# Batch 0's softmax and norm reworked at the head of a fused attention and feed-forward kernel: squares from products of the states, transposes by TensorE, a new first order

## The chip, the cores and the metric

The kernel runs on one core of one Trainium2 chip. A core has TensorE (PE, matmuls[...]), VectorE (DVE), ScalarE (ACT), GpSimd (POOL) and SyncE (SP), each with its own instruction queue that is worked off in order, and 16 DMA engines that all queues share. The metric is the device time of one launch in microseconds (us), as the median of several runs. The profiled execution has a span, from the first to the last instruction of the core, and a time that is a little longer.

## What is computed

The reference, cut to what matters (all in float32; eight batches, eight heads of 64, 512 tokens and 32 states per batch):

```python
def _attn_ref(x, state):                     # x (8, 8, 512, 64), state (8, 8, 32, 64)
    scale = 1.0 / np.sqrt(D)
    a = softmax(scale * x @ state.T)         # with max, and sum + 1e-09
    xread = a @ state
    a2 = softmax(scale * state @ x.T)
    sread = a2 @ x
    return np.concatenate([xread, sread], axis=2)

def _moe_ref(x, w_gate, w_val, w_out, rms_g):   # x (4352, 512), widths 512 -> 1536 -> 512
    rms = np.sqrt(np.mean(x * x, axis=-1, keepdims=True) + 1e-06)
    xn = x / rms * rms_g
    g = xn @ w_gate
    return (g / (1.0 + np.exp(-g)) * (xn @ w_val)) @ w_out
```

The norm needs, for each token, the mean square of `xread` over all heads. The weights arrive as 64-bit floats.

## The kernel before

The attention output of the tokens is never formed. A token's row of `xread` is `a` (32 values per head) times the states, so the kernel multiplies the states into the weights (`own_weights`) and applies the softmax values `a` to the result. What it needs of `xread` itself is its length, for the norm.

Of the eight batches, batch 0 is done in a first stretch of its own, together with the conversion of the weights from 64 bit and with the attention of batch 1. From batch 1 on each batch is one period, and the states are last. What stands on PE, DVE, ACT, POOL and SP, and in which order, is written out by hand: strings of letters (`ORDER` for the first stretch, then `FIRST`, `PERIOD`, `LAST`, `STATES`), where each letter takes one step of one generator. In `ORDER`, `a` and `s` are the reads of batch 0 (`tokens_read`, `states_read`), `A` and `S` those of batch 1, `e` and `d` the two halves of the weight conversion (`exponents` on ACT, `values` on DVE), `v` is `own_weights`, `h`, `t` and `u` are the hidden layer of batch 0 (matmuls on PE, silu on ACT, gating on DVE), `p` is its projection, `c`, `k` and `w` prepare batch 1, and `z` is `keep_awake`, one 128x256 matmul that computes nothing (L1149).

The weights come in 18 pieces: for each of six pairs of hidden blocks one of `w_gate`, one of `w_val` and one of `w_out`. A piece is loaded as raw 64-bit data (`load_piece`, four pieces ahead), takes three ACT steps (L234, L236, L239) and four DVE steps (L260, L263, L267, L272), each over 128x1024 elements; piece 0 is cut in two halves. `own_weights` (L567) needs the converted `w_gate` and `w_val` of its pair, `project_as_ready` (L817) the converted `w_out`.

Batch 0's path runs so. Scores: the states are transposed (L307, copied by DVE at L310), x is transposed in four chunks (L318, copied by ACT at L320), and the scores (L345) come out with the 32 states of four heads on the partitions, in two PSUM banks, `e` = 0 and 1. DVE transposes them in 32x32 blocks (L354) so that the states lie along the free dimension, takes the maximum (L414) and subtracts it (L416); ACT takes the exponential (L418); DVE sums (L426), inverts (L428, L429), scales (L431) and transposes back (L433) into `aT_s`. ACT keeps a copy of the scores for the states' own read (L358).

Norm: PE forms the token reads (L440, `aT_s` times the states) in four banks, ACT squares them (L447), DVE adds the four (L450), PE sums over the partitions (L367), DVE adds the small constant (L371), POOL takes the power -1/2 (L289), PE spreads the result over the rows (L296), and DVE scales `aT_s` by it (L453). Only then can the first matmul of the hidden layer (L610) start. The matmuls of L610, L817 and L567 then fill PE up to the first product of batch 1 (L714).

The start of the loads: SP issues the states of batch 0, chunks 1 and 3 of x, `rms_g` and then the weight pieces; ACT issues chunks 0 and 2 of x:

```python
    load_state(0)
    load_x(0, nc.scalar, nc.sync)
    nc.sync.dma_start(out=rms_g, in_=moe_rms_g.rearrange("(i p) -> p i", p=P))
    load_piece(0)
```

PSUM has eight banks; the pools are `aps` and `vps` (two each, tiles `at` and `pv`), `fx` (two), `fy` and `fz` (tiles `f`).

Of the kernel before, what the change touches and what calls it, by code (L numbers as in the profile page):

```python
# [22 lines left out]
    "zzzzzzzzzzazadaaaaaaaaazzzdzzzzzzeaeeaaaaadaadeeaaaaeeezdeazdzzzzzzadeeeaadaadzz"  # L23
    "zzzzzzzaaaaaddadzzzzvvvaaedzaAAdaaassdAAAAaAAeeAaAhtddddehehhuppedddddvtduppeeee"
    "ddvvdddeeeedAAddhhtuhhpeAddeApAtddeesvuvddveApdddhheedtupddeeehtAAAddhueeeddsApA"
    "AAdpepvvevAsddddedddphtsssseeehuhAdtssddpdshuedeedpvvvAeApdeAehtdhhAueddppAdddtA"
    "eeddpAheuSSAAAeAAvAvvpehhtSSddhdAAASSpAtuSShSSSdkAuwwsSSSpcpcskpwckkkkkkkkpwkkwc"
    "wwww"
# [29 lines left out]
def kernel(  # L58
# [137 lines left out]
    def load_piece(k):  # L196
        if k >= len(pieces):
            return
        src = pieces[k]
        if src.dtype == F32:  # L200
            return
        raw[k] = raws.tile([P, 8 * P, 2], I32, name="raw")
        out_ = raw[k].rearrange("p (a f) two -> p a (f two)", a=src.shape[1])
        for a in parts(k):
            nc.sync.dma_start(out=out_[:, a], in_=src[:, a].bitcast(I32))

# [85 lines left out]
    def along_rows(ri, n):  # L292

        rp = aps.tile([P, NC, P], F32, name="at")
# [7 lines left out]
    def scores(b, packed, soft):  # L302
# [8 lines left out]
        yield "step"  # L311

# [40 lines left out]
        for e in range(2):  # L353
# [7 lines left out]
        soft.update(st=stT, e=eS)  # L361

    def rms_on_array(b, sq):

        sp = aps.tile([P, NC], F32, name="at")
        for c in range(NC):
            TE.matmul(out=sp[:, c:c + 1], lhsT=sq[:, 0, P * c:P * c + P], rhs=ones,  # L367
                      start=True, stop=True)
# [6 lines left out]
        rp = along_rows(ri, NC)  # L375
# [27 lines left out]
    def tokens_read(b):  # L403
# [6 lines left out]
        def along(t, e):  # L410
            return t[:, e].unsqueeze(2).to_broadcast([P, S // Ns, Ns])

        for e in range(2):
            VE.reduce_max(out=m1[:, e], in_=eS[:, e], axis=AXX)  # L414
            yield
            VE.tensor_tensor(out=eS[:, e], in0=eS[:, e], in1=along(m1, e), op=ALU.subtract)  # L416
# [8 lines left out]
        for e in range(2):  # L425
# [7 lines left out]
            VE.transpose(out=aT_s[b][:, e], in_=eS[:, e].rearrange("p k n -> p (k n)"))  # L433
# [3 lines left out]
        reads = [(aps, vps)[j // 2].tile([P, S], F32, name=("at", "pv")[j // 2]) for j in range(4)]  # L437
        for j in range(4):
            for e in range(2):
                TE.matmul(out=reads[j][D * e:D * e + D, :],  # L440
                          lhsT=packed[Ns * j:Ns * j + Ns, e, :],
                          rhs=aT_s[b][Ns * j:Ns * j + Ns, e],
                          start=True, stop=True)
        yield
        sq = one.tile([P, 4, S], F32, name="sq", tag="xT")
        for i, j in enumerate((2, 3, 0, 1)):
            SE.activation(out=sq[:, i, :], in_=reads[j], func=ACTF.Square, scale=DM ** -0.5)  # L447
            yield "step" if i == 3 else None
        for i, j in ((0, 1), (2, 3), (0, 2)):
            VE.tensor_tensor(out=sq[:, i, :], in0=sq[:, i, :], in1=sq[:, j, :], op=ALU.add)  # L450
            yield
        rp = yield from (rms_on_array if b < 2 else rms_on_blocks)(b, sq)
        VE.tensor_tensor(out=aT_s[b], in0=aT_s[b],  # L453
                         in1=rp.unsqueeze(1).to_broadcast([P, 2, S]), op=ALU.mult)
# [100 lines left out]
    def own_weights(b, mp):  # L555
# [4 lines left out]
        def products():  # L560
            w = w_sb.pop(b * (NM // 2) + mp)
            for e in range(2):
                pv.append(vps.tile([P, 4 * P], F32, name="pv") if b and mp % 2 == 0 else
                          aps.tile([P, 4 * P], F32, name="at"))
# [601 lines left out]
    parts_0, banks_0 = {}, []  # L1166
    load_state(0)
    load_x(0, nc.scalar, nc.sync)
    nc.sync.dma_start(out=rms_g, in_=moe_rms_g.rearrange("(i p) -> p i", p=P))
    load_piece(0)  # L1170
    for k in range(1, RAW_AHEAD):
        load_piece(k)
# [76 lines left out]
```

## Time and profile before

| | us |
|---|---|
| median of three runs | 762.73 |
| lowest, highest | 762.08, 765.21 |
| the profiled execution | 762.78 |
| its span | 760.5 |
| PE busy | 747.2 (98%) |
| DVE busy | 600.3 (79%) |
| ACT busy | 351.1 (46%) |
| POOL busy | 294.0 (39%) |
| first hidden product of batch 0 (L610) starts | 36.27 |
| first product of batch 1 (L714) starts | 136.78 |

The times of engines are from the page of the profile, the two starts from the timeline of PE. A float32 matmul appears as two records, so "x8" in a row stands for four matmuls. In the timeline a row gives the start, the length, the engine, the line, the tiles and in brackets how long the engine had been idle and what released it. The busy share of PE contains the matmuls of `keep_awake`, which are work for the profile but not for the result.

### The profile page before, as it was taken

To read this page: it belongs to the slowest core of one execution; us is meant where nothing else is said; L and a number is where in the kernel's file an instruction comes from. 1 tells how busy PE (TensorE), PEld (TensorE's weight loads), DVE (VectorE), ACT (ScalarE), POOL (GpSimd) and SP (SyncE) were. 2 spreads that over 40 slices of the span, in tenths; PEclk is the share of its full clock that TensorE was granted. 3 is DMA by queue.
4 is the path that set the end of the run, shared out by engine and by line. 5 is a ranking of instruction groups with operands and counts; after the bars stand their busy time and mean duration, and the time that the engine had idled before them with its cause. 6 is when DMAs were issued, how large, how long until landed. Compare 5 with 4: busy or idle time off the path is not lost.

```text
span 760.5 us, 14354 instructions
## 1 busy us (share of the span) xinstructions
PE 747.2 (98%) x5608; PEld 595.3 (78%) x5608; DVE 600.3 (79%) x1000; ACT 351.1 (46%) x548; POOL 294.0 (39%) x379
## 2 busy tenths in 40 slices
PE   8899999999899999999999999999999999999998
PEld 6534435678778798879877997889788987899997
DVE  3999997679956898589947994799579975787961
ACT  4898974553225532654155424553355236411220
POOL 2000002893675325542374038312843266323700
PEclk9999999999999999999999999999999999999999
DMA  9787754695576266834774376617662756133411
GB/s 291 214 277 264 289 214 162 231 305 178 195 234 242 56 244 214 297 78 181 256 245 151 125 267 219 222 40 306 217 228 39 293 184 241 56 90 119 140 56 28
DMA packets 61890, 146.15 MB, mean 192 GB/s; under 512 B 15744, under 2 KB 32640, under 8 KB 54912
## 3 DMA queue, kind: packets, MB, share of 16 engines
q1 hardware_dynamic: 48704, 125.78, 47.3%
q10 hardware_dynamic: 13120, 19.47, 9.0%
q8 instruction: 44, 0.72, 0.4%
q14 instruction: 22, 0.18, 0.1%
HBM read 116.46 MB, written 28.77 MB: 191 GB/s over the span
## 4 chain that ended last, share of the span: by engine, by line
PE 88%; DVE 8%; POOL 1%; ACT 1%; issue 1%; DMA 0%; SPq 0%; ACTq 0%; POOLq 0%; DVEq 0%
PE f L714 36%; PE f L1017 27%; PE f L817 6%; PE pv L610 5%; PE at L567 3%; PE pv L567 2%; PE f L880 2%; PE at L345 1%; PE f L1149 1%; PE at L509 1%; PE at L440 1%; DVE hb L1076 1%; DMA out_dram<-kept 0%; PE at L296 0%; DVE hb L790 0%
## 5 line engine op out<-in xcount | busy, mean ns | idle before, releaser
L714 PE MATMUL f<-aT_s,v 128*128 128x256 f32 x504 | 119.6, 382 | 0.0
L714 PEld LDWEIGHTS f<-aT_s,v 128*128 128x128 f32 x504 | 94.5, 190 | 24.8 <-issue 9.2
L777 DVE TENSOR_TENSOR g<-g,f 128x512 f32<-128x512 f32 x84 | 57.3, 685 | 42.6 <-PE f L714 38.6
L1043 POOL TENSOR_TENSOR kept<-kept 128x256 f32<-128x256 f32 x28 | 23.1, 826 | 175.0 <-DVE kept L1057 173.6
L714 PE MATMUL f<-aT_t,vs 128*128 128x256 f32 x336 | 87.2, 383 | 0.3 <-ACT g L761 0.3
L1027 ACT COPY kept<-f 128x512 f32<-128x512 f32 (+1 forms) x56 | 29.7, 532 | 124.8 <-PE f L1017 83.0
L1017 PE MATMUL f<-w,h 128*128 128x128 f32 x588 | 74.6, 276 | 1.0 <-DVE h L1067 1.0
L714 PEld LDWEIGHTS f<-aT_t,vs 128*128 128x128 f32 x336 | 62.4, 190 | 16.0 <-POOL vs L594 4.2
L1017 PEld LDWEIGHTS f<-w,h 128*128 128x128 f32 x588 | 69.6, 192 | 5.4 <-issue 4.1
L768 ACT ACTIVATE hb<-g 128x1024 f32<-128x1024 f32 x42 | 44.5, 1058 | 56.7 <-DVE g L777 56.6
L594 POOL TENSOR_TENSOR vs<-v 128x256 f32<-128x256 f32 x42 | 31.7, 755 | 80.4 <-ACT v L579 80.4
L289 POOL TENSOR_TENSOR ri<-ss,mhalf 128x4 f32<-128x4 f32 x8 | 10.4, 1295 | 124.5 <-DVE ss L371 114.6
L766 ACT COPY g<-f 128x512 f32<-128x512 f32 x42 | 24.6, 586 | 44.5 <-PE f L714 44.5
L714 PE MATMUL f<-aT_t,v 128*128 128x256 f32 x168 | 43.5, 381 | 1.6 <-DVE c L777 1.6
L817 PE MATMUL f<-wo,hb 128*128 128x512 f32 x96 | 44.4, 600 | 0.0
L610 PE MATMUL pv<-aT_s,v 128*128 128x512 f32 x96 | 43.7, 597 | 0.3 <-ACT t L616 0.3
L714 PE MATMUL f<-aT_s,vs 128*128 128x256 f32 x168 | 43.6, 382 | 0.0
L790 DVE TENSOR_TENSOR hb<-hb,c 128x512 f32<-128x512 f32 (+1 forms) x48 | 36.9, 768 | 8.0 <-ACT hb L768 7.3
L790 DVE TENSOR_TENSOR hb<-hb,f 128x512 f32<-128x512 f32 (+1 forms) x48 | 31.0, 646 | 15.0 <-PE f L714 15.0
L1017 PE MATMUL f<-wo,h 128*128 128x128 f32 x336 | 42.2, 275 | 0.0
L1017 PE MATMUL f<-wo,hb 128*128 128x128 f32 x336 | 42.1, 275 | 0.0
L777 DVE TENSOR_TENSOR c<-c,f 128x512 f32<-128x512 f32 (+1 forms) x48 | 31.2, 650 | 12.6 <-PE f L714 12.5
(183 smaller groups left out, 1689.1 us busy)
## 6 DMA issues: line engine op xcount, KB each, us to landing
w_m<-w_d SPq DMA_DIRECT2D x48, 1024.0 KB, 5.9
w<-t_d SPq DMA_DIRECT2D x49, 576.0 KB, 5.4
out_dram<-kept SPq DMA_DIRECT2D x56, 128.0 KB, 2.1
raw<-in_moe_w_val_dram SPq DMA_DIRECT2D x6, 1024.0 KB, 5.5
raw<-in_moe_w_out_dram SPq DMA_DIRECT2D x6, 1024.0 KB, 7.1
w_d<-w_m SPq DMA_DIRECT2D x6, 1024.0 KB, 4.9
x_b<-in_x_dram SPq DMA_DIRECT2D x6, 1024.0 KB, 7.5
x_d<-xB ACTq DMA_DIRECT2D x6, 1024.0 KB, 4.2
```

The source lines that it names most:

```text
L567: TE.matmul(out=pv[e][Ns * j:Ns * j + Ns, :], lhsT=stT_g[b][D * e:D * e + D, j, :], rhs=w[D * e:D * e + D, j].rearrange("p m k f -> p (m k ...
L594: GE.tensor_tensor(out=vs[:, 0], in0=a21, in1=a22, op=ALU.add)
L610: TE.matmul(out=to[0], lhsT=lhs(i, k), rhs=r, start=(i == 0), stop=(i == len(rhs) - 1))
L714: TE.matmul(out=ps[:, i, 0:half], lhsT=l[:, i, :], rhs=r, start=(start and i == 0 and k == 0), stop=(k == len(lhs) - 1), skip_group_check= ...
L766: SE.copy(gates(q)[1], q["x"][:, :, 0:half])
L768: SE.activation(out=hb[:, 2 * mp:2 * mp + 2, 0:n].rearrange("p m (c t) -> p m c t", c=2), in_=q["g"][:, :, :, 0:half], func=ACTF.Silu if s ...
L777: VE.tensor_tensor(out=to, in0=to, in1=q[ps][:, :, 0:half], op=ALU.add)
L790: VE.tensor_tensor(out=part, in0=part, in1=val, op=ALU.mult)
L817: TE.matmul(out=banks[r], lhsT=hb[:, m, P * r:P * r + P], rhs=wo[:, m, :], start=(m == 0), stop=(m == NM - 1))
L1017: TE.matmul(out=to[half][:, slot, :], lhsT=lhs[:, k, :], rhs=rhs[:, k, :], start=(fresh and n in (0, 4) and k == 0), stop=(k == QM - 1), s ...
L1027: SE.copy(k[:, 4 * i:4 * i + 4 - i], banks[name][i])
L1043: GE.tensor_tensor(out=k[:, 1:3], in0=k[:, 0:1].to_broadcast([P, 2, QD]), in1=k[:, 1:3], op=ALU.add)
```

## The change

Five things are changed, all for batch 0 and in the first stretch.

1. The mean square of a token's read is taken without forming the read. With G = states times states, transposed (32x32 per head, divided by 512, the `gram` tile), the sum of squares of a head is the sum over its states of a * (G a). PE forms G once (8 small matmuls) and then G a (`ga`), DVE multiplies by `aT_s`, and the sum over the partitions takes both halves (8 matmuls of one column). The four squares on ACT and the three additions on DVE are gone for batch 0.
2. The four transposes in 32x32 blocks on DVE are replaced for batch 0 by 128x128 transposes on PE. The first ones read the copy that ACT makes of the scores; maximum and subtraction then read PSUM. The second ones are copied to `aT_s` by ACT.
3. The last scaling of `aT_s` is done in two halves.
4. The first half of weight piece 0 is issued on SP ahead of all else; ACT issues chunks 0 and 1 of x, SP chunks 2 and 3; `rms_g` comes after piece 1.
5. `ORDER` is dealt anew, and some PSUM tiles of batch 0 come from other pools. 13 `z` instead of 10 stand ahead of the first transpose, 14 instead of 31 after the scores; four transposes of x of batch 1 stand after the first hidden products instead of before them.

The other order strings are as before. The core of the diff:

```diff
@@ scores
+        if b == 0:
+            gp = [vps.tile([P, Ns], F32, name="pv") for e in range(2)]
+            for j in range(4):
+                for e in range(2):
+                    st = stT[D * e:D * e + D, j, :]
+                    TE.matmul(out=gp[e][Ns * j:Ns * j + Ns, :], lhsT=st, rhs=st, start=True, stop=True)
+            yield
+            gram = soft["gram"] = x_0.tile([P, 2, Ns], F32, name="gram")
+            for e in range(2):
+                VE.tensor_scalar(gram[:, e], gp[e], 1.0 / DM, None, op0=ALU.mult)
+            yield "step"
...
-        for e in range(2):
+        soft.update(st=stT, e=eS, raw=[eS[:, e] for e in range(2)])
+        for e in range(2) if b == 0 else ():
+            SE.copy(sS[:, e].rearrange("p c t -> p (c t)"), sp[e])
+            yield
+            tp = vps.tile([P, NC, P], F32, name="pv")
+            for c in range(NC):
+                TE.transpose(out=tp[:, c, :], in_=sS[:, e, c, :], identity=ident)
+            soft["raw"][e] = tp.rearrange("p c (j n) -> p (c j) n", n=Ns)
+            yield "step" if e else None
+        for e in range(2) if b else ():
             VE.transpose(out=eS[:, e].rearrange("p k n -> p (k n)"),
@@ tokens_read
-            VE.reduce_max(out=m1[:, e], in_=eS[:, e], axis=AXX)
+            VE.reduce_max(out=m1[:, e], in_=soft["raw"][e], axis=AXX)
             yield
-            VE.tensor_tensor(out=eS[:, e], in0=eS[:, e], in1=along(m1, e), op=ALU.subtract)
+            VE.tensor_tensor(out=eS[:, e], in0=soft["raw"][e], in1=along(m1, e), op=ALU.subtract)
...
+            tp = aps.tile([P, NC, P], F32, name="at")
+            for c in range(NC):
+                TE.transpose(out=tp[:, c, :], identity=ident,
+                             in_=eS[:, e, 4 * c:4 * c + 4].rearrange("p j n -> p (j n)"))
+            yield
+            SE.copy(aT_s[b][:, e], tp.rearrange("p c t -> p (c t)"))
             yield "step"
...
+        if b == 0:
+            sq = one.tile([P, 2, S], F32, name="sq", tag="xT")
             for e in range(2):
+                ga = vps.tile([P, S], F32, name="pv")
+                for j in range(4):
+                    here = slice(Ns * j, Ns * j + Ns)
+                    TE.matmul(out=ga[here, :], lhsT=soft["gram"][here, e, :], rhs=aT_s[b][here, e],
+                              start=True, stop=True)
+                yield
+                VE.tensor_tensor(out=sq[:, e, :], in0=aT_s[b][:, e], in1=ga, op=ALU.mult)
+                yield "step" if e else None
...
-        VE.tensor_tensor(out=aT_s[b], in0=aT_s[b],
-                         in1=rp.unsqueeze(1).to_broadcast([P, 2, S]), op=ALU.mult)
+        for e in (slice(0, 2),) if b else (slice(0, 1), slice(1, 2)):
+            VE.tensor_tensor(out=aT_s[b][:, e], in0=aT_s[b][:, e],
+                             in1=rp.unsqueeze(1).to_broadcast([P, e.stop - e.start, S]), op=ALU.mult)
@@ loads
+    halves = load_parts(0)
+    next(halves, None)
     load_state(0)
-    load_x(0, nc.scalar, nc.sync)
+    load_x(0, nc.scalar, nc.scalar, nc.sync, nc.sync)
+    for _ in halves:
+        pass
+    load_piece(1)
     nc.sync.dma_start(out=rms_g, in_=moe_rms_g.rearrange("(i p) -> p i", p=P))
-    load_piece(0)
-    for k in range(1, RAW_AHEAD):
+    for k in range(2, RAW_AHEAD):
         load_piece(k)
```

`load_parts(k)` is `load_piece(k)` as a generator that issues one part of the piece at each step.

## Prediction

> **What bounds the kernel now.** I read the page first: TensorE (PE) is busy 98% of the span and has 88% of the chain that ended last. Such a share leaves almost nothing to win except where PE is kept busy with work that nobody needs, so I then asked for the busy time by stage. The order of instructions per engine, compared between the two kernels, is the same from the first product of batch 1 on (the group `f<-aT_s,v` of L714); all that changes lies before it. In the trace that first product starts at 136.78 us.
>
> ```profile
> core 0: us, PE busy (x) PEld busy (x) DVE busy (x) ACT busy (x) POOL busy (x), PEclk, DMA share, GB/s
> 0.00:36.30 36.30, 31.93 (x179) 23.20 (x179) 24.54 (x42) 22.95 (x32) 6.00 (x28) 1.00 0.92 264
> 36.30:136.80 100.50, 100.17 (x512) 42.35 (x511) 92.42 (x121) 79.67 (x100) 6.18 (x8) 1.00 0.68 240
> ```
>
> From 36.30 to 136.80 us PE works 100.17 of 100.50 us: that stage cannot shrink unless matmuls go. Before 36.30 PE is busy too, but with what? The timeline of PE tells:
>
> ```profile
> 8.15 0.27 PE L307 MATMUL at<-ident,rows 128*128 128x128 f32 x1
> ...
> 11.79 1.09 PE L345 MATMUL at<-xT,stT 64*32 64x512 f32 x16 [0.68 <-ACT xT L320]
> 12.81 11.49 PE L1149 MATMUL f<-ident 128*128 128x256 f32 x52
> ...
> 33.93 0.65 PE L296 MATMUL at<-ident,ri 128*128 128x128 f32 x4 [0.45 <-POOL ri L289]
> 34.41 0.60 PE L318 MATMUL at<-ident,x_b 128*128 128x128 f32 x4
> 35.69 0.66 PE L318 MATMUL at<-ident,x_b 128*128 128x128 f32 x4 [0.68 <-ACT xT L320]
> 36.27 3.70 PE L610 MATMUL pv<-aT_s,v 128*128 128x512 f32 x8
> ```
>
> The L1149 matmuls (52 records, 26 matmuls, 0.442 us each) are the idle-time filler. So the first 36 us are the latency of batch 0's softmax and norm, and VectorE (DVE) sets it. Its timeline, from scores to the scaled softmax that L610 waits for:
>
> ```profile
> 12.97 1.31 DVE L354 STREAM_TRANSPOSE eS<-at 128x512 f32<-128x512 f32 x2 [1.84 <-PE at L345]
> ...
> 24.62 0.70 DVE L433 STREAM_TRANSPOSE aT_s<-eS 128x512 f32<-128x512 f32 x1
> ...
> 28.75 1.29 DVE L450 TENSOR_TENSOR sq<-sq 128x512 f32<-128x512 f32 x2
> ...
> 35.01 1.21 DVE L453 TENSOR_TENSOR aT_s<-aT_s,at 128x1024 f32<-128x1024 f32 x1
> ```
>
> DVE has no idle note between those lines: 22 us of back-to-back work, a good part of it the conversion of weight pieces (L260 to L272). Last the waits of PE inside the dense stage, and SP's queue at the start:
>
> ```profile
> PE pv L610 <- ACT t L616: 0.3, 1, 0.3
> ```
>
> ```profile
> 2.57 1.06 SPq L137 DMA_DIRECT2D x_b<-in_x_dram  x2
> 4.17 1.07 SPq L1169 DMA_DIRECT2D rms_g<-in_moe_rms_g_dram  x1
> 5.29 1.20 SPq L205 DMA_DIRECT2D raw<-in_moe_w_gate_dram  x2
> ```
>
> The norm weights' DMA takes 1.07 us to issue where its neighbours take about 0.5; the wait of SP there is 0.5 us, for the first chunk of x, so that chunk landed at about 4.7 us.
>
> **What the skill says.** "TensorE: Matmul & The Clock Gate", Part 1, has PE at half clock until about 3.4 us of sustained work and again after an idle window of about 3.4 us. The trace agrees for the start: the filler runs at about 0.8 us a matmul until some 5 us and at 0.44 later; no hole before L610 is over 1 us, so no return to the slow clock is seen. "DMA: Bandwidth & Descriptors", section on queues and rings, says that each DMA engine takes turns between the rings packet by packet; a large load on SP therefore delays one that ScalarE (ACT) issues at the same moment. No run here shows that case yet. DVE reads of PSUM (g<-g,f, 685 ns) and of SBUF (0.69 us) cost the same in this trace, so moving a source to PSUM is put at nothing.
>
> **The change, part by part.** Instructions on DVE follow each other at less than their duration; from the timeline I take 0.61 us for a 128x512 op (0.68 if it needs the one before), 1.14 for 128x1024, 0.34 to 0.7 for `top`, 0.45 for the z pair with its reciprocal.
>
> *Start.* 13 filler matmuls stand ahead of the first transpose instead of 10, at 0.442: stT's copy moves from 8.46 to 9.79 us and ends at 10.08. The Gram matmuls are new: 8 of 32x32. The trace has no such shape; L509's small tiles bound it below (64 records in 1.10 us, so 0.3 for 16), L345's tiles of the same position with 16 times the columns above (1.09 us for 16 records). I take 0.5 to 0.9 (the latency of the last one and of its semaphore included), so x's transposes begin at 10.55 to 10.95 instead of 8.85. From there to L345 was 2.94 us, to the scores in PSUM 1.18 more: 14.7 to 15.1, against 12.97. Loss so far 1.7 to 2.1 us. The first half weight piece is what this buys: it has landed by about 6 us (4.7 us after issue, as before), so its three ACT and first two DVE steps are done before x; before, DVE waited for it to 9.97 and ACT's share stood at 11.63 to 13.9.
>
> *Scores to softmax.* Gone from DVE: four 512-wide transposes (2 x 0.65 of scores, 2 x 0.62 of aT) and three additions (1.9), 4.5 us. Added: two products with the Gram result (1.2), one maximum moved ahead (0.6), two tiny evictions off the path. The transposes now run PE -> ACT or ACT -> PE: sS copy 0.57, four transposes 0.45, and eS is read from PSUM. DVE then goes without a hole: sS max 15.35 to 15.75, max e0 15.95, subtract 16.6, max e1 17.2, ex 17.85, subtract 18.45, stT_g 19.05, sum 19.25, weight 19.85, z 20.45, scale e0 20.9, sum 21.5, z 22.1, scale e1 22.6, `top` 23.2, man 23.9, sq e0 25.05, ex 25.65, sq e1 26.8, weight 27.4, ss 28.55 (low ends; high ends are 0.4 later). The aT copy of e1 is queued on ACT behind two weight steps (1.15 each) and comes at 24.8, its product at 26.4, ahead of sq e1: covered by 0.4 us. Without that cover each late us of ACT is a us of the path.
>
> *Norm to L610.* POOL's power 1.0 us, four transposes 0.6: ready at 30.3. But DVE has `top`, sS max, man, stT of batch 1 and ex of piece 2 queued ahead (3.8 us from 28.55): the scaling starts at 32.35, its first half (now split) ends at 33.0, and the first hidden product starts at 33.05 to 33.45, mean 33.25, against 36.27. That is 3.0 us earlier. Four transposes of x of batch 1 (0.53) now come after it instead of before, which gives 0.5 back; the 0.34 us wait for `t` goes, since ACT's table load and first silu (36.0 to 36.6) end before the second pair needs the bank (37.6).
>
> *Dense stage.* The same matmuls as before otherwise: 100.17 + 0.53 = 100.7 from 33.25 gives 133.95 for the first batch-1 product, against 136.78: 2.8 us. This needs DVE and ACT to stay ahead. DVE starts its conversions 2.7 us earlier with the same list after it, so the last w_m of the sixth pair, which before ended at 111.2 for a matmul at 111.94, ends near 108.3 for one at 109.1. ACT has two places where DVE waits for it (0.6 us each, at the seventh silu and at the 14th piece): inside the 0.8 us of slack.
>
> *Loads.* SP puts half a piece (about 0.55 us of issue) ahead of the state and two chunks of x; ACT now issues chunks 0 and 1. The rotation of eight DMA semaphores makes chunk 3 wait for chunk 0's landing, 4.7 us before and up to 1.3 later now (512 KB at the 400 GB/s the timeline shows once large rows flow): issue at about 6, landing (3.4 to 5.2 after issue) at 9.5 to 11.5. Its transposes are due at 12.5. So it is hidden by 1 us or more. All later loads shift by under 1 us and have over 3.
>
> *Later batches.* Same order; their waits are relative to PE, so the 2.8 us stays. 762.78 less 2.8 is 760.0 for the profiled execution; the median shown is 0.05 lower: 759.9. The span would be 757.7.
>
> **Rivals.**
> (1) More than that: every unknown at its low end (Gram matmuls 0.3, ops at 0.6 throughout, scaling at 31.5 to 31.9) and the c3 transposes falling into waits of PE. The first product at 32.2, gain 4.1: 758.6. For it: the DVE sums made with single durations came out about 1.5% above the stretch from 35 to 110 us. Against: the path has few places with play.
> (2) The start eats it: chunk 3 lands at about 14.5 instead of 11, because big packets stand between the small ones of x. Then L610 moves 2 us and some 0.8 us are left: 761.9. Against: the margin above.
> (3) Slower: PE's clock. Between the transposes of e1 and the first hidden product PE has holes (about 1.7 us before the second Gram product, shorter ones after), with little filler between. If PE drops to half clock there, it enters the dense stage slow; each window of 3.4 us costs 1.7 us of matmuls. Two windows cost 3.4, a third of a us more for the transposes on the path: 759.9 + 3.8 = 763.7. It decides from the second window; over 0.5% slower needs four. Against: the longest hole is half a window.
> (4) The dense stage starves: a pair of w_m late by more than 0.8 us. Each us is one us; 1.5 late gives 761.4.
>
> **How the numbers follow.** 0.5% (3.8 us) is about what a measurement of this kernel can tell from no change. Chances: forecast 0.53, (1) 0.24, (2) and (4) 0.14, (3) 0.09, of which 0.05 beyond 0.5%, to which (4) adds 0.01. The forecast's own range is 759.2 to 760.8; with (1), (2) and most of (4) it reaches from 757.8 to 762.3. Faster by over 0.5% is (1) and the edge of the forecast: 0.28. Slower 0.06, within 0.5% 0.66.
>
> **What would show it.** The first transpose of the states at 9.5, the scores' matmuls at 13.7, the first scaled aT at 33, the first hidden product at 33.3, no wait of PE over 0.5 us up to the first product of batch 1, and that at 134. A wait of PE for x at 11 to 14 us shows (2); a low granted clock or 0.8 us fillers after 20 us shows (3); PE waiting for w_m shows (4). If the first product comes at 134 and the span shrinks by something else, the later batches are not as independent as I took them to be.

## The result, and the profile after

| | before | after |
|---|---|---|
| median of six runs each on one chip | 763.65 | 759.85 |
| lowest, highest | 762.08, 765.21 | 759.33, 760.79 |
| the profiled execution | 762.78 | 759.33 |
| its span | 760.5 | 757.5 |
| first hidden product of batch 0 (L610, now L658) | 36.27 | 33.82 |
| first product of batch 1 (L714, now L762) | 136.78 | 134.30 |
| from the first of these to the second | 100.51 | 100.48 |

The ratio of after to before is 0.9953, with a 95% interval from 0.9934 to 0.9972. The forecast was 759.9. The two medians lie 3.8 us apart, the two profiled spans 3.0 and the first hidden products 2.45: which of these is the gain is taken up in the part on the prediction.

The busy time by stage of the changed kernel shows at once where the gain lies. The columns are the window, its length, then busy time and number of instructions of PE, of the weight loads (PEld), of DVE, ACT and POOL, then the granted clock of PE, the DMA share and GB/s.

```profile
0.00:33.60 33.60, 28.25 (x184) 19.64 (x184) 21.77 (x38) 21.26 (x29) 7.15 (x28) 1.00 0.96 256
33.60:134.20 100.60, 100.49 (x516) 42.90 (x514) 92.24 (x121) 80.26 (x101) 7.50 (x9) 1.00 0.70 249
```

The second stretch is as full as before and as long as before; the first is shorter. So the question is the first 34 us only. The timeline of PE in the changed kernel:

```profile
9.80 0.27 PE L310 MATMUL at<-ident,rows 128*128 128x128 f32 x1
10.45 0.29 PE L321 MATMUL pv<-stT 64*32 64x32 f32 x16 [0.39 <-DVE stT L313]
10.68 1.09 PE L333 MATMUL at<-ident,x_b 128*128 128x128 f32 x8
...
13.83 1.09 PE L360 MATMUL at<-xT,stT 64*32 64x512 f32 x16 [0.67 <-ACT xT L335]
...
26.08 1.06 PE L477 MATMUL pv<-aT_s,gram 32*32 32x512 f32 x8 [0.45 <-ACT aT_s L467]
27.07 2.24 PE L391 MATMUL f<-ones,sq 128*128 128x1 f32 x16
...
31.29 0.65 PE L299 MATMUL pv<-ident,ri 128*128 128x128 f32 x4
...
33.82 3.70 PE L658 MATMUL pv<-aT_s,v 128*128 128x512 f32 x8
```

The Gram matmuls (L321) take 0.29 us, and from the states' transpose to the scores 4.0 us pass, against 3.6 before (8.15 to 11.79). The scores are therefore 2.0 us later than before, and the first hidden product is nevertheless 2.45 us earlier: between the two, 4.5 us were saved. DVE, whose list of work stands between the two:

```profile
4.96 0.53 DVE L263 TENSOR_SCALAR top<-raw 128x512 int32<-128x512 int32 x1 [4.96 <-DMA raw<-in_moe_w_gate_dram]
...
15.63 0.69 DVE L513 TENSOR_REDUCE m<-sS 128x1 f32<-128x512 f32 x1 [2.11 <-ACT sS L370]
...
29.34 0.16 DVE L396 TENSOR_SCALAR ss<-f 128x4 f32<-128x4 f32 x1
...
31.95 1.21 DVE L270 SCALAR_TENSOR_TENSOR ex<-raw,ex 128x1024 int32<-128x1024 int32 x1
33.08 1.28 DVE L500 TENSOR_TENSOR aT_s<-aT_s,pv 128x512 f32<-128x512 f32 x2
```

The first half of weight piece 0 is there at 4.96 us. From 15.63 to the scaling DVE has no idle note in its timeline. The sum of squares (`ss`) comes at 29.34 against 32.62 before; the norm is then ready on PE at about 32, but the scaling (L500) stands behind five steps of other work and starts at 33.08.

Some 2.4 of the 4.5 us were not saved but moved. Four conversion steps of piece 0 that stood behind the scores in the kernel before (L267, L272, L260 and L263, at 15.49, 16.69, 18.69 and 19.39, 2.42 us in sum) now stand ahead of them (at 11.04, 11.76, 12.37 and 12.82), in time that DVE spends waiting anyway. The rest is what fell away on DVE, transposes and additions, less what came in.

Of the waits of PE from 33 to 136 us one line is left, and the wait for `t` that the kernel before had is gone:

```profile
PE at L333 <- ACT xT L335: 0.2, 1, 0.2
```

### The profile page after: what moved, and what is told of

It is laid out like the page before. It is cut to its first block, busy times and chain, and to the rows that moved or that the text cites. A ratio compares the mean times of both kernels' runs of the same rounds, so it can differ in the third digit from the quotient of the medians.

```text
span 757.5 us, 14370 instructions
## 1 busy us (share of the span) xinstructions
PE 743.8 (98%) x5618; PEld 592.5 (78%) x5618; DVE 599.3 (79%) x998; ACT 350.1 (46%) x546; POOL 295.2 (39%) x379
## 4 chain that ended last, share of the span: by engine, by line
PE 91%; DVE 7%; issue 1%; ACT 1%; POOL 0%; DVEq 0%; POOLq 0%
PE f L762 37%; PE f L1065 28%; PE f L865 6%; PE pv L658 6%; PE at L615 3%; PE pv L615 3%; PE f L928 2%; PE f L1197 1%; PE at L556 1%; PE at L360 1%; PE at L486 1%; DVE hb L1124 1%; PE at L299 0%; DVE hb L838 0%; DVE eS L456 0%
## 5 line engine op out<-in xcount | busy, mean ns | idle before, releaser
L762 PE MATMUL f<-aT_s,v 128*128 128x256 f32 x504 | 119.6, 382 | 0.0
L762 PEld LDWEIGHTS f<-aT_s,v 128*128 128x128 f32 x504 | 94.5, 190 | 24.8 <-issue 8.4
L1091 POOL TENSOR_TENSOR kept<-kept 128x256 f32<-128x256 f32 x28 | 23.1, 824 | 174.9 <-DVE kept L1105 173.8
L762 PE MATMUL f<-aT_t,vs 128*128 128x256 f32 x336 | 87.1, 383 | 0.0
L762 PEld LDWEIGHTS f<-aT_t,vs 128*128 128x128 f32 x336 | 62.5, 190 | 15.3 <-POOL vs L642 4.2
L762 PE MATMUL f<-aT_t,v 128*128 128x256 f32 x168 | 43.5, 381 | 1.6 <-DVE c L825 1.6
L658 PE MATMUL pv<-aT_s,v 128*128 128x512 f32 x96 | 43.9, 595 | 0.1
L762 PE MATMUL f<-aT_s,vs 128*128 128x256 f32 x168 | 43.6, 382 | 0.0
L838 DVE TENSOR_TENSOR hb<-hb,c 128x512 f32<-128x512 f32 (+1 forms) x48 | 36.7, 764 | 8.0 <-ACT hb L816 7.2
```

Source lines behind the costliest of these rows:

```text
L658: TE.matmul(out=to[0], lhsT=lhs(i, k), rhs=r, start=(i == 0), stop=(i == len(rhs) - 1))
L762: TE.matmul(out=ps[:, i, 0:half], lhsT=l[:, i, :], rhs=r, start=(start and i == 0 and k == 0), stop=(k == len(lhs) - 1), skip_group_check= ...
L838: VE.tensor_tensor(out=part, in0=part, in1=val, op=ALU.mult)
L1091: GE.tensor_tensor(out=k[:, 1:3], in0=k[:, 0:1].to_broadcast([P, 2, QD]), in1=k[:, 1:3], op=ALU.add)
```

## The experiments

The theory to be tested has two parts. *The head alone sets the time*: everything after the first hidden product runs as before, so a change of its start passes one to one into the time. *DVE's queue sets the head*, with what it waits for. The rival is the third one of the prediction: PE's clock. In all kernels the same function is computed, and none leaves work out. HP is the start of the first hidden product and FB that of the first product of batch 1, both from the timeline of PE in the profiled execution. The mean granted clock (by the record of cores) belongs to that execution; median and ratio to before, with its interval, are over all timed runs (their number in brackets). The ratio is the one on record and is not the quotient of the two medians: for e12 that would be 760.54 to 762.17, or 0.998.

| kernel | HP | FB | FB−HP | clock | median | ratio to before |
|---|---|---|---|---|---|---|
| e1 squares as before | 39.61 | 139.96 | 100.35 | 0.993 | 765.33 (20) | 1.0029 [1.0017, 1.0042] |
| e2 transposes as before | 38.63 | 139.01 | 100.38 | 0.991 | 763.90 (12) | 1.0007 [0.9994, 1.0021] |
| e3 loads as before | 36.89 | 137.30 | 100.41 | 0.996 | 761.86 (20) | 0.9989 [0.9977, 1.0001] |
| e4 10 fillers at the start | 33.61 | 133.98 | 100.37 | 0.998 | 760.00 (7) | 0.9953 [0.9934, 0.9973] |
| e5 4 fillers more in the holes | 34.94 | 135.43 | 100.49 | 1.0 | 760.91 (21) | 0.9976 [0.9966, 0.9987] |
| e6 e4 and e5 together | 33.74 | 134.23 | 100.49 | 0.999 | 760.55 (11) | 0.9980 [0.9967, 0.9992] |
| e7 e1 with 8 fillers | 35.64 | 136.05 | 100.41 | 0.998 | 761.39 (20) | 0.9990 [0.9983, 0.9997] |
| e8 e2 with 16 fillers | 35.97 | 136.47 | 100.50 | 1.0 | 762.21 (12) | 0.9995 [0.9983, 1.0008] |
| e9 scaling one step ahead | 33.55 | 134.37 | 100.82 | 1.0 | 760.57 (21) | 0.9975 [0.9965, 0.9985] |
| e10 e4 with one filler | 32.51 | 133.00 | 100.49 | 0.998 | 758.06 (6) | 0.9933 [0.9911, 0.9956] |
| e11 before, new loads | 36.47 | 136.96 | 100.49 | 0.999 | 762.37 (20) | 1.0003 [0.9991, 1.0015] |
| e12 changed, again | 34.73 | 135.09 | 100.36 | 0.998 | 760.54 (15) | 0.9962 [0.9948, 0.9975] |

e1 to e4, e5 to e8 and e9 to e12 ran on one chip each, with medians of before of 762.43, 761.96 and 762.17. In thirteen of the fourteen traces FB−HP lies between 100.35 and 100.51 (e9 is treated below), while HP goes from 32.5 to 39.6. Up to FB the first part of the theory is shown: a change of HP passes on unchanged. From FB to the end of the span it holds less well. There the fourteen traces take 623.0 to 625.3 us, a spread nearly as large as the gain. In e5 and e7 some 1.5 us of it lie behind the last matmul, in the issue of the last output transfers (first line the changed kernel, second e5); in e10 a stretch of slow clock lies in a later batch, as is shown below.

```profile
754.52 0.85 ACTq L1180 DMA_DIRECT2D out_dram<-h  x2
756.26 2.40 ACTq L1180 DMA_DIRECT2D out_dram<-h  x2
```

One thing more moves HP by some tenths. The same 13 fillers at the start take 8.50 us in the first trace of the changed kernel and 8.09 in e12, which has the same program, so that the states' transpose starts at 9.80 in the one and at 9.39 in the other. Where two traces are compared below, this start is given if it differs.

### Parts of the change taken out: e1, e2, e3

e1 forms the token reads again, squares them on ACT and adds on DVE; the order string was adapted.

```diff
-        if b == 0:
-            gp = [vps.tile([P, Ns], F32, name="pv") for e in range(2)]
...
-                VE.tensor_tensor(out=sq[:, e, :], in0=aT_s[b][:, e], in1=ga, op=ALU.mult)
+        for i, j in enumerate((2, 3, 0, 1)):
+            SE.activation(out=sq[:, i, :], in_=reads[j], func=ACTF.Square, scale=DM ** -0.5)
+            yield "step" if i == 3 else None
+        for i, j in ((0, 1), (2, 3), (0, 2)):
+            VE.tensor_tensor(out=sq[:, i, :], in0=sq[:, i, :], in1=sq[:, j, :], op=ALU.add)
```

> The changed kernel with the squares of before: eight matmuls form batch 0's reads, ACT squares four banks, DVE adds three times; the Gram products are gone, all else is as changed. Main theory (the moment at which the first hidden product can start sets the whole time, and DVE and ACT queues set that moment): four squares on ACT (2.1 us) and three additions (1.9) stand in for two products (1.2), and the additions wait for the squares. First hidden product 1.0 to 2.0 us later than the changed kernel's 33.82 us, first product of batch 1 and the span later by the same, so about 761 us. Rival (the gain is from the new order and the early load, the arithmetic being covered by other work): within 0.3 us of the changed kernel.

e2 puts the four transposes back on DVE and keeps the rest; here too the order string was adapted. Of the code, the part on the second two:

```diff
-            tp = aps.tile([P, NC, P], F32, name="at")
-            for c in range(NC):
-                TE.transpose(out=tp[:, c, :], identity=ident,
-                             in_=eS[:, e, 4 * c:4 * c + 4].rearrange("p j n -> p (j n)"))
-            yield
-            SE.copy(aT_s[b][:, e], tp.rearrange("p c t -> p (c t)"))
+            VE.transpose(out=aT_s[b][:, e], in_=eS[:, e].rearrange("p k n -> p (k n)"))
```

> The changed kernel with the block transposes of DVE for batch 0 in place of those of TensorE; the Gram products and the loads stay. Main theory: the first two fall into a hole of DVE at 13.5 to 15.6 us but push the first maximum of sS behind them (0.6), the last two (1.25) are added to DVE's closed queue, while the ACT copies and their latency go: first hidden product 1.2 to 2.0 us later than 33.82, the span by the same. Rival (DVE is not what sets that moment): no later, or earlier by up to 0.5 us, since a copy of ACT and the waits of TensorE for it are gone.

e3 has the old order of loads under the new order of everything else.

```diff
-    halves = load_parts(0)
-    next(halves, None)
     load_state(0)
-    load_x(0, nc.scalar, nc.scalar, nc.sync, nc.sync)
-    for _ in halves:
-        pass
-    load_piece(1)
+    load_x(0, nc.scalar, nc.sync)
     nc.sync.dma_start(out=rms_g, in_=moe_rms_g.rearrange("(i p) -> p i", p=P))
+    load_piece(0)
+    load_piece(1)
```

> The changed kernel with the loads issued as before (states, x, rms_g, then the weights; x dealt in turn to ACT and SP). Main theory: the first half piece lands at about 10 us, and the copy of the transposed states is queued on DVE behind its first two steps (1.1 us), so it comes at 11.1 instead of 10.11; ACT's three steps end at 12.1 in front of the first copy of x. First hidden product 0.8 to 1.2 us later, the span by the same. Rival (the early load itself buys nothing, the order does): within 0.3 us.

All three moved HP further than had been expected from DVE's durations: 5.8, 4.8 and 3.1 us. The timeline of PE of e1 shows why (in the changed kernel the 16 records of the own-weights product, L591 here, take 1.09 us and four filler records 1.03):

```profile
30.77 1.87 PE L379 MATMUL f<-ones,sq 128*128 128x1 f32 x8 [3.88 <-DVE sq L472]
...
32.74 1.91 PE L1173 MATMUL f<-ident 128*128 128x256 f32 x4
34.59 1.96 PE L591 MATMUL f<-w_m,stT_g 64*32 64x512 f32 x16
```

After a hole of 3.88 us the four filler records take 1.91 us instead of 1.03, and L591 1.96 instead of 1.09. The busy time by windows of e1 gives the clock:

```profile
28.10:31.50 3.40, 0.73 (x4) 0.73 (x4) 2.58 (x4) 3.37 (x5) 0.00 (x0) 0.50 0.90 297
31.50:34.90 3.40, 3.40 (x19) 2.48 (x26) 2.23 (x5) 0.77 (x1) 1.02 (x1) 0.50 0.90 330
34.90:38.30 3.40, 3.40 (x25) 1.82 (x10) 1.66 (x3) 0.59 (x1) 0.00 (x0) 0.50 0.00 0
38.30:41.70 3.40, 3.18 (x14) 1.81 (x13) 3.37 (x5) 3.20 (x5) 0.00 (x0) 0.99 0.16 18
```

The clock is 0.50 for three whole windows, then full. e2 has it too, for four windows, from 23.1 to 36.7 us, after a hole of 3.77 us:

```profile
23.67 1.93 PE L460 MATMUL pv<-aT_s,gram 32*32 32x512 f32 x8 [3.77 <-DVE aT_s L450]
```

e3 has two separate stretches, from 11.3 to 14.7 and from 31.7 to 35.2. So rival 3 is no mere possibility, and e1 to e3 measure two things at once: the part of the change, and the clock that the removed part had kept up. They don't tell the worth of a part at full clock.

### The same parts with the clock kept up: e5, e7, e8

Fillers were put into the holes: in e5 two ahead of the second Gram product and two ahead of the sum over the partitions, in e7 eight after the token reads, in e8 sixteen at three places. The code of e7 and e8 is that of e1 and e2; only letters of `ORDER` are added, in e5 so:

```diff
-    "aaadaaeAdadsdeezezAdavaaAvAAAAvhehteeAeAdddduhhppdAddtdeeedvvvudeeedphhdtheeddtA"
+    "aazzadazzaeAdadsdeezezAdavaaAvAAAAvhehteeAeAdddduhhppdAddtdeeedvvvudeeedphhdthee"
...
```

> The changed kernel with four more idle-time matmuls, two ahead of the second Gram product and two ahead of the sum over the partitions, where TensorE waits anyway. Clock theory (several runs of the changed kernel have a mean granted clock of 0.996 to 0.998 because TensorE does too little between 22 and 30 us and is put on half clock for one or two stretches of 3.4 us just before the dense stage): more of the runs at clock 1.0, median 0.3 to 0.8 us lower than the changed kernel's 759.85 (span 757.5 to 757.8 at clock 1.0), spread narrower. Rival (the lower mean clocks have another place or cause): clocks and times as the changed kernel's.

> The kernel of e1 (squares of before, all else changed) with eight idle-time matmuls in the hole of 3.9 us that TensorE had between the reads and the sum. If the clock was only a companion there: no half clock at 28 to 38 us, the first hidden product at 35 to 36 us (1.2 to 2.2 after the changed kernel's), first product of batch 1 at 135.6 to 136.5, span 759 to 760. Rival (the arithmetic alone costs the 5 to 6 us that e1 showed): first hidden product at 38 to 39.5 at full clock as well.

> The kernel of e2 (block transposes of DVE, all else changed) with 16 idle-time matmuls in the holes that TensorE had there. At full clock: first hidden product at 35.5 to 36.3 us (DVE's transposes cost 1.7 to 2.5), first product of batch 1 at 136 to 136.8, span 759.3 to 760.2. Rival (DVE's transposes cost the 4.8 us that e2 showed): first hidden product at 38 to 39.

The clock is back: e1 never had a run above 0.996 and e2 none above 0.991, e7 and e8 none below 0.997. HP of e7 is 35.64 and of e8 35.97, that is 4.0 and 2.7 us earlier than without the fillers, although these cost PE time:

```profile
35.64 3.60 PE L634 MATMUL pv<-aT_s,v 128*128 128x512 f32 x8
35.97 3.70 PE L642 MATMUL pv<-aT_s,v 128*128 128x512 f32 x8
```

Against the changed kernel's 33.82 the Gram products are worth 1.8 us of HP and the transposes on PE 2.15 us, or 2.5 if it is counted that e8 started 0.4 earlier (9.41 against 9.80). The fillers seem to delay nothing here: after them PE still waits 0.23 us for DVE in e7, and DVE has no idle note from 15.99 us to the scaling in e8. The times agree in direction: the ratios of e7 and e8 lie above that of e12, with intervals that do not touch, though they were taken on another chip.

In the changed kernel itself the same remedy is too dear. None of the 21 runs of e5 has a clock below 0.997, as the clock theory had it, but the median did not fall. The timeline of PE of e5:

```profile
24.58 1.06 PE L477 MATMUL pv<-aT_s,gram 32*32 32x512 f32 x8
25.57 1.13 PE L1197 MATMUL f<-ident 128*128 128x256 f32 x4
26.63 1.06 PE L477 MATMUL pv<-aT_s,gram 32*32 32x512 f32 x8
27.62 1.13 PE L1197 MATMUL f<-ident 128*128 128x256 f32 x4
```

The second Gram product starts at 26.63 instead of 26.08, with a hole of 0.45 us before it filled by two fillers of 1.13 us in sum. The sum, which had no hole before it, follows at 28.59 instead of 27.07 and ends at 30.43 instead of 29.31. HP loses the same 1.1 us.

### The early load: e3 and e11

e11 is the kernel before with the new loads alone; its edit is that of e3 the other way round, with `load_parts` added.

> The kernel before with the loads' order of the changed kernel alone: half of weight piece 0 first on SP, ACT issues chunks 0 and 1 of x, SP chunks 2 and 3, the norm weights after piece 1. The order of everything else is that of before. Main theory (the early half piece pays only where the order of DVE and ACT puts its steps ahead of x): the first hidden product stays within 0.3 us of 36.27 and the time within 0.4 us of that of the kernel before. Rival (the early landing pays by itself, because DVE waited for the first piece to 9.97 us in the kernel before): the first hidden product starts 0.8 us or more earlier, and the time falls by as much. Third: the later chunk 3 of x delays the scores, and the time grows by 0.5 us or more.

HP is 36.47 and the ratio 1.0003 [0.9991, 1.0015]: by itself the early load buys nothing. The timeline of DVE of e11 shows where it goes:

```profile
8.83 0.42 DVE L264 TENSOR_SCALAR top<-raw 128x512 int32<-128x512 int32 x1
...
13.13 1.31 DVE L358 STREAM_TRANSPOSE eS<-at 128x512 f32<-128x512 f32 x2 [3.15 <-PE at L349]
```

The old order has the states' copy first and the scores after; the 1.1 us (8.83 against 9.97) only lengthen the wait for the scores, from 1.84 to 3.15 us. In the new order without the early load (e3) HP, at 36.89, is later than in both kernels with the old order (36.27 and, in e11, 36.47). The timelines of DVE and ACT of e3:

```profile
9.66 0.43 DVE L263 TENSOR_SCALAR top<-raw 128x512 int32<-128x512 int32 x1 [9.66 <-DMA raw<-in_moe_w_gate_dram]
...
10.73 0.28 DVE L313 COPY stT<-at 128x128 f32<-128x128 f32 x1
```

```profile
9.66 0.68 ACT L237 ACTIVATE ex<-raw 128x512 f32<-128x512 f32 x1 [6.51 <-DMA raw<-in_moe_w_gate_dram]
...
12.45 0.59 ACT L335 COPY xT<-at 128x512 f32<-128x512 f32 x1 [0.48 <-PE at L333]
```

The weight steps stand ahead of the states' copy and of the copies of x, and the piece lands at 9.66. The copy of the states, whose transpose had been done at 8.9, waits to 10.73; the first copy of x follows at 12.45 against 11.37. Just after the hole of 2.17 us that PE has there, the first stretch of half clock begins. The scores come at 15.62 against 13.83, and `ss` at 31.13 against 29.34.

Of these 1.8 us only 0.6 are the late copy of the states; most of the rest is slow clock, for the 16 records of x take 3.64 us in one run. So the load buys nothing without the order, but the opposite is not shown. Three of the 20 runs of e3 had clock 1.0 and took 759.98 to 760.35 us, 1.9 less than the 35 runs of the kernel before at clock 1.0 beside it (median 762.21). That is the same distance as for e12 (759.89, five runs, against 761.77, 32 runs). What the early load adds when the clock holds is not settled by so few runs; in the traces its lack comes with a hole and with slow clock.

### The start: e4, e6, e10, and the changed kernel again, e12

The changed kernel puts 13 fillers ahead of the states' transpose. e4 takes three of them out, e6 adds to that the four of e5, e10 adds to e4 one filler ahead of the second Gram product. e12 is the changed kernel. The edit of e10:

```diff
-    "ddzzzzzzzzzezzzeezaaaaaaaaaaaaddaezddaseaaazzaeaaazzdaaaazdeezzzazzaaaazeeaaaadd"
-    "aaadaaeAdadsdeezez...
+    "ddzzzzzzzzzeeezaaaaaaaaaaaaddaezddaseaaazzaeaaazzdaaaazdeezzzazzaaaazeeaaaaddaaz"
+    "adaaeAdadsdeezez...
```

> The changed kernel with 10 instead of 13 idle-time matmuls ahead of the first transpose. Main theory: every step up to the first hidden product moves 1.3 us earlier and so does the end, to about 758.5 us, unless x is late: chunk 3 is then needed at 11.2 us and was issued at about 6, so a wait of TensorE for it of up to 0.5 us may eat part. Rival (x and the states arrive only just in time and the 13 are no cost): no change.

> The same four, and 10 instead of 13 ahead of the first transpose. Main theory and clock theory together: the first hidden product at about 32.4 us at full clock, first product of batch 1 at 132.9, the span 756.0, the median near 758. Rival (clock): as with ten and no fillers, a median near 760 with runs at a clock of 0.995.

> The changed kernel with 10 fillers instead of 13 ahead of the first transpose of the states, and one filler put ahead of the second Gram product; all else is the same. Of the kernel with 10 fillers alone the runs at full clock were at 757.7 to 757.9 and the others at 760 to 761. Main theory (the start gains about 1.3 us, and what takes it away is the half clock of PE in the hole ahead of the second Gram product and after it): with the hole halved the clock of the runs is above 0.998 more often, the first hidden product starts at 32.4 to 33.0, and the median is 758.2 to 759.3, below the changed kernel on the same chip by 0.7 to 1.5 us. Rival (half clock comes from the sum of small matmuls and pauses, and one filler does not stop it): clocks as with 10 fillers alone, first hidden product at 33.5 to 33.8, median 759.8 to 760.5.

> The changed kernel itself, unaltered, beside the three others: what its time is on this chip, and how often its runs have a mean clock below 0.998. Expected from its first six runs: median 759.3 to 760.2; runs at clock 1.0 at 759.3 to 759.6, those at 0.996 about 1.2 us higher. If the clock alone makes the spread, time and mean clock go together over all runs; if they do not, the spread has another cause.

e4 gained at the start and lost it again. Its first transpose starts at 8.27 us, but then the clock goes to one half, from 28.6 to 32.0 us, and HP is 33.61. Two of its seven runs had clock 1.0 and took 757.73 and 757.86 us. e12 tells that this is not peculiar to e4. The timeline of PE of e12:

```profile
25.67 1.06 PE L477 MATMUL pv<-aT_s,gram 32*32 32x512 f32 x8 [0.45 <-ACT aT_s L467]
26.66 2.23 PE L391 MATMUL f<-ones,sq 128*128 128x1 f32 x16
...
29.85 1.96 PE L615 MATMUL f<-w_m,stT_g 64*32 64x512 f32 x16
31.74 1.11 PE L299 MATMUL pv<-ident,ri 128*128 128x128 f32 x4
```

L615 takes 1.96 us and L299 1.11, nearly twice what they took in the first execution (1.09 and 0.65). The windows of e12:

```profile
26.40:29.80 3.40, 3.27 (x25) 2.60 (x21) 3.39 (x6) 2.26 (x3) 0.63 (x1) 1.00 0.41 148
29.80:33.20 3.40, 3.40 (x24) 1.69 (x24) 3.26 (x5) 2.06 (x3) 0.77 (x1) 0.51 1.00 317
```

The same program lost a stretch of its clock in one profiled execution and none in the other, and HP is 34.73 instead of 33.82; as e12 had started 0.4 earlier, the stretch cost 1.3 us of HP. Over e12's 15 runs the clock was 1.0 in five, with a median of 759.89, and from 0.995 to 0.999 in ten, from 759.36 to 762.22. The median of 760.54 is above the 759.3 to 760.2 that had been expected. Clock and time go together in the main, not strictly: the lowest time has 0.998. One reason is in the trace of e7, whose clock of 0.998 comes from the end of the span alone: its last matmul ends at 755.7, and the clock is one half from 757.7 on. Slow clock there delays no matmul, so a mean clock a little below 1 does not tell by itself that time was lost.

e10 has the lowest median of all. HP is 32.51, 1.3 us ahead of the changed kernel; the states' transpose starts at 8.49. Four of its six runs had clock 1.0 and 757.18 to 758.37 us, two 0.998 and 759.09 and 759.51. Those four are below the lowest of e12's 15 runs. The medians differ by 2.5 us, where HP explains 1.3; with six runs the size is not settled, and the intervals of the ratios overlap ([0.9911, 0.9956] and [0.9948, 0.9975]). Nor is it shown that the one filler is what keeps the clock. The two runs of e4 at full clock are as fast as the four of e10, so the earlier start comes from the 10 fillers in both; full clock in four runs of six against two of seven can be chance. One filler of 0.44 us in a hole of 0.45 moves the second Gram product by 0.1 us at most: it starts at 24.88, 1.2 ahead of 26.08, where the states' transpose is 1.3 ahead. e6, with four of them, has its HP at 33.74 instead of the expected 32.4 and throws most of the gain away.

The profiled execution of e10 had its half clock stretch elsewhere, in the second period. The timeline of PE there:

```profile
201.08 1.45 PE L1065 MATMUL f<-w,hb 128*128 128x128 f32 x6
202.32 2.66 PE L1065 MATMUL f<-w,h 128*128 128x128 f32 x12
```

Twelve records take 2.66 us there; the same form took 1.60 at 193.7. So not all the spread of the times comes from the head. The kernel before has a spread of this kind too: 14 of its 51 runs beside e12 had a clock of 0.993 to 0.996 and took some 3 us more than the rest. Where in the kernel their clock was lost no trace shows, as its profiled execution was one at clock 1.0.

### No slack behind the head: e9

The scaling was moved ahead of the `ex` step of piece 2 on DVE.

```diff
-    "aaadaaeAdadsdeezezAdavaaAvAAAAvhehteeAeAdddduhhppdAddtdeeedvvvudeeedphhdtheeddtA"
+    "aaadaaeAdadsdeezezAavaadAvAAAAvhehteeAeAdddduhhppdAddtdeeedvvvudeeedphhdtheeddtA"
```

> The changed kernel with one pair of DVE steps exchanged in the first order: the scaling of aT_s by the norm (L500, two halves) stands ahead of the 512-wide ex step of weight piece 2 (L270, 1.21 us) instead of behind it. All else is the same, and so is what is computed. Main theory (the head is DVE's queue, and DVE's conversions have no slack left in the second pair): the first hidden product starts 1.1 us earlier, at 32.7 against 33.82, but the w_m steps of the second pair, which end at about 44.6 for an own-weights product at 44.76 in the changed kernel, do not come earlier, so that PE waits 0.7 to 1.0 us there; the stretch from the first hidden product to the first product of batch 1 grows from 100.48 to 101.2 to 101.5, that product starts at 133.9 to 134.3, and the time moves by 0 to 0.4 us. Rival (the start of the hidden layer alone sets the time): the stretch stays at 100.4 to 100.5, the first product of batch 1 starts at 133.2, and the time falls by 1.1 us.

The time is that of e12 beside it, 760.57 and 760.54, as the main theory expected, but not in the way it described. The scaling starts 1.1 us earlier, at 31.98. HP does not follow: it is 33.55 and not 32.7. The timeline of PE of e9:

```profile
33.06 0.66 PE L333 MATMUL at<-ident,x_b 128*128 128x128 f32 x4 [0.24 <-ACT xT L335]
33.55 3.60 PE L658 MATMUL pv<-aT_s,v 128*128 128x512 f32 x8
...
37.43 3.88 PE L658 MATMUL pv<-aT_s,v 128*128 128x512 f32 x8
```

Four transposes of x of batch 1 stand ahead of the hidden product and wait for a copy by ACT to 33.06. PE was a second limit 0.27 us behind DVE. And that 0.27 is given back at once: the second group takes 3.88 us instead of 3.60, because a weight load of it waits for the gating on DVE, which did not come earlier (it starts at 38.58, in the changed kernel at 38.41):

```profile
39.32 0.30 PEld L658 LDWEIGHTS pv<-aT_s,v 128*128 128x128 f32 x2 [0.84 <-DVE hb L668]
```

The w_m of the second pair, where the loss was expected, comes only after that: its product starts at 44.81 against 44.76 before the exchange. So the second part of the theory holds only in part. In e8, where work went back to DVE and DVE has no pause up to the scaling, HP is later; but in the changed kernel PE and ACT limit HP only 0.27 us behind DVE. Moving one step of DVE gains no more than that; in e10 everything came earlier together.

## Why the prediction came out right

**The total.** 757.7 was forecast for the span, 757.5 was profiled. It is a sum of parts that were off by some tenths in both directions: HP came 0.6 late, the dense stage was 0.2 shorter, and 0.5 came in from the later batches, for which there was no reason in the forecast. That the median, 759.85, meets the 759.9 is luck. The forecast counted 2.8 us from the kernel before at 762.73, but the six runs beside the changed kernel have it at 763.65, a difference of 3.8; e12 and the runs beside it differ by 1.6 in their medians, and by 1.9 if only runs at clock 1.0 are taken. The 2.8 lies between these. What was right is the way: a shorter head, DVE's list as its measure, and a dense stage that keeps its length.

**Start.** The states' copy was put at 9.79 and came at 10.11 (0.3 late, within the 0.4 by which the start varies between two executions). The Gram matmuls with their latency were put at 0.5 to 0.9, so that x would begin at 10.55 to 10.95; it began at 10.68. The first maximum was put at 15.35 to 15.75 and came at 15.63. The fillers of the kernel before, said to run slowly to some 5 us, did so somewhat longer: stretches of 0.85 us hold one matmul up to 5.7 us, stretches of 0.43 from 6.2 on. The half piece came at 4.96 instead of 6, which can have moved nothing, as DVE stood idle for 3.90 us after its first two steps.

**Scores to softmax.** The list was right in its order and its count, but too tight: `ss` was put at 28.55 to 28.95 and came at 29.34. Of the 0.8 us above the low end, 0.3 are there at the first maximum, 0.4 at the next one (16.34 against 15.95), which follows the end of PE's transposes at 16.31, and 0.5 at the subtraction that needs it (17.07 against 16.6); the rest is spread. The copy of e1 was put at 24.8 and its product at 26.4, 0.4 ahead of its turn on DVE at 26.8. The copy came at 25.44, the product ended at 27.14, and DVE came at 27.52, so the cover held with all three about 0.7 late.

**Norm to the hidden product.** The 3.8 us of queued work after `ss` were 3.74. The scaling came at 33.08 instead of 32.35, the whole of it inherited, and HP at 33.82 instead of 33.05 to 33.45: outside that range by 0.4.

**Dense stage.** 100.7 was forecast and 100.48 measured; no wait of PE was left. That the later batches keep the gain was right within what the traces can tell: from FB to the end of the span it is 623.2, and 623.7 before, and the same stretch varies by more than that among the experiments. A wait of 0.3 us for ACT at about 390 us, there in the kernel before, is missing in the changed one; the rest is not traced.

**Loads.** A chunk of x waited on SP for the landing of another one, as expected of chunk 3; the view names the tensor and not the chunk. The waits of the DMA queue of SP, changed kernel:

```profile
SPq L136 <- DMA x_b<-in_x_dram: 2.4, 1, 2.4
```

Its issue was over by 6.4 us, and no wait of PE for x appears in the timeline. Rival 2 did not happen.

**Rival 3** was priced nearly right and judged wrongly. Summed over slices of 0.1 us, the clock missing in e4, in e10 and in e12 is 1.707 us each, and in e1 and e2 three and four times that. This is half of a window of 3.41 us, as the forecast had it, but it is clock and not time. In the head, where PE also waits, HP of e12 lost 1.3 us by it, and e4 is as far behind e10 when their starts are counted (8.27 and 8.49). But the argument against it, that the longest hole is half a window, does not hold. Whether a stretch falls into the head differs from one execution to the next: the trace that the forecast was held against had none. In e12 no hole from 24 to 30 us is longer than 0.45. "TensorE: Matmul & The Clock Gate" of the Trainium skill, Part 1, gives an idle window of about 3.4 us as the condition, and says that the window runs free, so that what falls into it differs from run to run. The lengths here (3.4 us and multiples) and the difference between two executions of one program agree with the second; the first is too narrow: the 3.40 us ahead of the drop in e12 have PE busy for 3.27 us in the trace. Two thirds of that are the products of one column (L391, 2.23 us), the rest fillers, a transpose and the end of the Gram product. That products of one column count as little activity would explain it; no run here tested it by itself. Clock below full is moreover no mark of the changed kernel alone: 10 of the 15 runs of e12 have it, and 19 of the 51 runs of the kernel before beside it, some of them perhaps only behind the last matmul.

**Rival 4** did not happen. In e9 PE did lose 0.28 us to DVE in the dense stage, but at the gating and not at a w_m. **Rival 1** needed all its low ends; HP came 1.6 us later than its 32.2. That a start of 32.5 can be had was shown by e10, by another way: fewer fillers.

## What to carry to other kernels

Before pricing what a shorter chain saves on an engine, compare its start and the start of the next full stage across two traces: if their distance stays the same, one number tells the change up to there, and what follows has to be looked at by itself. Work taken off TensorE in a stage where it already waits can cost clock; look at the granted clock and at the length of a known instruction after the hole, not only at the hole, and fill a hole with no more than fits in it. An early load gains nothing until the order of the engines uses it (e11), so the two are to be tried together, and each alone, with the clock looked at.

## What had not been expected of the hardware

Half clock came after windows in which the trace shows PE busy for 96% of the time (3.27 of 3.40 us, e12), and two executions of one program differ in it. It comes in whole windows of 3.4 us, four of them in e2, and takes 1.7 us of clock a window, of which the head of e12 lost 1.3 us of time. A window that the trace shows full does not end it at once: in e1 PE is busy for 3.40 of 3.40 us from 31.5 to 34.9, and the next window is at half clock again. And DVE reads its source from PSUM at nearly the price of SBUF also in a maximum of the same form, first line the kernel before from SBUF, second the changed kernel from PSUM:

```profile
14.20 0.65 DVE L414 TENSOR_REDUCE m<-eS 128x16 f32<-128x512 f32 x1
16.34 0.69 DVE L439 TENSOR_REDUCE m<-pv 128x16 f32<-128x512 f32 x1
```

The maximum of the other half takes 0.68 us in both kernels (16.09 and 17.67), and the subtraction 0.69 and 0.68 in both.
